# Attention and adapters on one core: the residual of nine row tiles is turned back by TensorE instead of by a transposing DMA

## The chip, the core and the metric

The kernel runs on one core of a Trainium2 chip. The metric is the device time of one execution in microseconds (us). Five engines work side by side, each with its own instruction queue: PE (TensorE, matrix products into PSUM; PEld are its weight loads), DVE (VectorE), ACT (ScalarE), POOL (GpSimd) and SP (SyncE). Here POOL only builds some constants and issues the input loads, SP issues stores and, before the change, transposing DMAs. Engines wait for one another through semaphores.

## What is computed

```python
def _attn_ref(q, k, v):                      # each (8, 12, 448, 64)
    scores = (1 / np.sqrt(64)) * np.matmul(q, k.transpose(0, 1, 3, 2))
    attn = np.maximum(scores, 0.0) ** 2 / 448
    return np.matmul(attn, v)

x = attn_out.transpose(0, 2, 1, 3).reshape(3584, 768)

def _moe_ref(x, w_gate, A, B):               # 8 experts of rank 16, the best 2 of each row
    logits = x @ w_gate
    # w: softmax over the two largest logits of a row
    # delta[row] = sum over its two experts e of w * (x[row] @ A[e]) @ B[e]
    return x + delta
```

So the output is the attention result x (3584 rows of 768) plus a small correction; x itself has to reach the output, row by row. It is this last part, the residual, that the change is about.

## The kernel before, in words

**Attention.** For each of 8 batches the 12 heads are worked in 3 "quads" of four heads. The inputs come by cast-loads from POOL's queue (`load`, L185, two DMAs of 112 KB for each q, k or v of a quad). TensorE turns q and k with an identity (`tp`, L313), a copy brings them to SBUF (`te`, L327 and L335). Then come 174 steps n: score products `qk` n (L452), relu n on ACT or DVE (L472, L474), squaring `sq` on DVE for two or three steps at a time (L489), and value products `pv` n (L520). Their result stands transposed, with the 64 head dimensions in the rows; copies `x` on ACT or DVE (L565) write it to `xt`, a tile of 128 rows by 6 blocks by 3584 columns in bf16. So x stands there turned: columns of `xt` are rows of the output.

**Adapters.** The 3584 output rows are 28 tiles of 128. Three tiles at a time go through the gate: `z` (L582, six products of each tile with the gate and A weights), a few small DVE steps (`gmax` to `gzp`), a transposing product `zt` in f32 (L644), and its copy `zT` (L661). Then each tile has two half tiles, `b` 2t and `b` 2t+1, each 384 columns wide, which sum residual and correction in a PSUM bank: three products of `xt` blocks with a bf16 identity (L728) turn x back, and a product of `zT` with B in f32 (L737; it is two instructions in the profile) adds the correction. A copy `o` (L773) on ACT or DVE brings the half to the tile `osb`, and a store `st` writes the rows (L783).

For nine of the 28 tiles (15 to 23, as three groups of three in `C["tg"]`) the kernel before does it otherwise: `turned` lets SP's queue issue six transposing DMAs for each group (L677, 18 in all), which write x turned back to a tile `xb`. Their half tiles then have only the product with B, and `o` is an add of PSUM and `xb` on DVE (L764):

```python
for x in range(0 if xb or xi else 3):
    nc.tensor.matmul(out=out(h)[:, x * 128 : x * 128 + 128],
                     lhsT=k.xt[:, 3 * h + x, c0 : c0 + 128], rhs=k.identb,
                     start=(x == 0), stop=False, skip_group_check=True)
...
nc.tensor.matmul(out=o, lhsT=T["zT", g0][:, zi], rhs=rhs,
                 start=xb is not None, stop=True, skip_group_check=True)
...
elif xb:
    nc.vector.tensor_add(osb()[...], out(h)[:, :W], T["xb", xb[1]][...])
...
else:
    cp(osb()[:, h * W : h * W + W], out(h)[:, :W])
```

**What sets the order.** No scheduler runs: the string `ORDER` lists all operations, with the engine after a colon (`:A`, `:D`) where there is a choice and the first PSUM bank after `@`. `ordered` walks through it and issues each operation on its engine, so the table fixes each engine's queue. Numbered words are n of `qk`, `relu`, `pv`, half tiles of `b` and `o`, and so on; words `f` are unnamed ones, mostly loads. Buffers come from pools of fixed size (`POOLS`), so a load on POOL can wait for PE to have finished with an older tile; a load also waits for the landing of the DMA issued eight before it.

TensorE works in two shapes here: `tp`, `qk` and `pv` address 64x64 quarters of its array, `z`, `zt` and `b` the whole. I call `b`, `z` and `zt` 128-row work, and a stretch of them between two 64-row operations a run.

Of the kernel before, what the change touches and what calls it, by code (L numbers as in the profile page):

```python
# [30 lines left out]
PARTS.update({7: ((0, 322, 1, (0, 1, 2)), (322, 448, 4, (0, 1, 2)))})  # L31


C = dict(late=6, xi=(), om=(), merge_x=0, sqp=((999, (2, 2, 3)),), om2=(), fl=(), gf=(), ai=4, tg=((15, 3), (18, 3), (21, 3)), sp=(), xbdur=1.45, bx=8, xh=2, apart=3, apcap=1, gl=(3, 1), tqlat=2.0)
GROUP = 2688
POOLS = dict(qT=5, a=11, zp=2, zT=3, osb=4, w=3, q=5, k=5, v=8, xb=3)


ORDER = """
f4 f3 f1 f0 f2 f6 f5 f8 f7 f11 f9 f10 f84@0 f12 f88 f85@2 f90 f89 f13 f87@4 qk0@6 f91 qk1@0 relu0:D qk2@2 f14  # L40
relu1:A qk3@4 relu2:D relu3:A tp2@6 f17 qk4@0 te2 relu4:A qk5@2 qk6@4 sq2 tp3@6 f16 relu5:A f86@0 te3 relu6:A
sq0 qk7@0 f15 qk8@2 qk9@6 relu7:A tp4@4 relu8:D relu9:A f18 qk10@0 te4 qk11@2 relu10:A qk12@6 sq4 tp5@4 f19
relu11:A qk13@0 relu12:A te5 tp6@2 f26 sq9 relu13:A qk14@4 qk15@6 tp7 relu14:A f23 sq7 pv0@0 pv1 pv2 relu15:A
pv3 qk16@4 te6 pv4 pv5 f20 relu16:A pv6 qk17@6 x13:D pv7@2 relu17:A qk18@4 sq11 f22 pv8 pv9 x12:A qk19@6
relu18:A pv10 qk20@0 relu19:D f21 pv11 relu20:A pv12 pv13 qk21@4 sq16 x27:A qk22@6 f27 qk23@0 relu21:A aw1@3
sq14 relu22:A f33 x26:D relu23:A qk24@4 tp8@6 ae1 f25 relu24:A sq18 qk25@0 qk26@2 tp9 relu25:A f55 pv14@4 pv15
pv16 te8 relu26:A pv17 qk27@0 f31 pv18 pv19 relu27:A pv20 sq23 qk28@2 qk29@6 x41:A f28 qk30@0 x40:D relu28:A
aw0@5 sq25 relu29:A f29 relu30:A qk31@2 ae0 tp10@6 tp11 f32 relu31:A sq21 qk32@4 qk33@0 relu32:A te10 pv21@2 f30
pv22 pv23 relu33:A qk34@4 sq30 qk35@6 relu34:A qk36@0 f37 relu35:D relu36:A qk37@4 pv24 pv25 relu37:A pv26 sq32
f35 qk38@6 tp12@0 pv27 relu38:A tp13 qk39@4 f43 x55:A te12 qk40@6 x54:A z0@3 relu39:A sq35 qk41@0 f34 z1  # L50
relu40:A qk42@4 relu41:D z2 relu42:A f38 qk43@6 gmax0 tp14@0 relu43:A sq28 qk44@4 tp15 f42 relu44:A gd0 qk45@6
gu0 te14 relu45:A qk46@4 f50 gt0 sq39 qk47@0 relu46:A pv28@6 pv29 pv30 gsg0 pv31 f24 relu47:A qk48@4 pv32 gw0
pv33 sq44 f48 pv34 relu48:A qk49@0 gzp0 x69:A f36 tp18@4 sq37 relu49:A tp19 pv35@2 zt0@7 zt1 zt2 x68:A f41 te18
qk50@0 zT0:A pv36 pv37 relu50:A qk51@6 sq46 pv38 pv39 f47 relu51:A pv40 qk52@4 qk53@0 pv41 relu52:A x82:D tp16@6
tp17 relu53:A te16 qk54@4 b2@2 relu54:A f44 sq49 qk55@0 o2:A qk56@6 qk57@4 relu55:A relu56:D b0@2 f49 x83:A
relu57:D qk58@0 o0:A qk59@6 f39 relu58:A z3@3 z4 sq51 relu59:A qk60@4 qk61@0 z5 f40 sq56 relu60:A b4@2 relu61:A
gmax3 qk62@6 f46 sq58 b1@4 relu62:A gu3 gd3 qk63@0 o4:A gt3 f65 sq42 qk64@6 gsg3 o1:A b3@5 relu63:A gw3 gzp3
b5@2 f51 relu64:A sq60 zt3@4 zt4 o3:A zt5 pv42@0 o5:A pv43 st2 qk65@6 zT3:A sq53 pv44 pv45 relu65:A qk66@2 st4
pv46 pv47 pv48 relu66:A tp20@4 st0 qk67@6 x96:D tp21 x97:A te20 f53 pv49@2 relu67:A pv50 qk68@0 pv51 pv52 sq63
relu68:A pv53 f66 pv54 pv55 qk69@4 qk70@6 x110:A relu69:D qk71@0 relu70:A f45 b6@2 x111:D relu71:A qk72@4 o6:D  # L60
tp22@6 relu72:A sq65 qk73@0 tp23 pv56@2 relu73:A pv57 f74 qk74@4 te22 pv58 pv59 relu74:A pv60 qk75@0 f79 pv61
sq67 pv62 relu75:A qk76@6 b8@4 f64 relu76:A x124:D qk77@0 x125:A sq70 tp24@6 relu77:A tp25 qk78@2 f59 z6@5 te24
relu78:A qk79@0 z7 relu79:A f52 o8:D qk80@2 qk81@6 sq72 z8 relu80:A b10@4 f54 gmax6 relu81:A sq77 qk82@0 tp26@2
o10:A tp27 qk83@6 relu82:A gd6 gu6 f56 b7@4 te26 relu83:A qk84@0 gt6 f70 o7:D qk85@2 gsg6 relu84:A qk86@6 gw6
sq74 b9@4 relu85:A pv63@0 pv64 relu86:A gzp6 pv65 qk87@2 pv66 sq79 pv67 relu87:A pv68 pv69 zt6@5 zt7 x138:D zt8
x139:A qk88@6 qk89@2 o9:A zT6:D qk90@0 relu88:A relu89:D st8 tp28@4 tp29 relu90:A f80 qk91@6 te28 pv70@2 pv71
relu91:A pv72 pv73 qk92@0 sq84 f60 pv74 pv75 relu92:A pv76 qk93@4 b14@6 x153:D x152:A f58 relu93:A sq81 qk94@0
tp30@2 o14:A tp31 pv77@4 relu94:A pv78 f77 qk95@6 te30 pv79 pv80 relu95:A pv81 qk96@0 pv82 f57 sq91 pv83
relu96:A qk97@2 b11@6 relu97:D x166:A f67 b12@7 x167:A o11:A sq93 qk98@0 st10 o12:A qk99@2 qk100@4 relu98:A
relu99:D b13@6 st6 relu100:A z9@7 sq88 qk101@0 o13:A tp32@2 qk102@4 relu101:A tp33 st12 b15@6 f62 sq86 relu102:A  # L70
qk103@0 o15:A te32 f61 qk104@4 relu103:A z10 z11 sq100 relu104:A qk105@2 f69 pv84@0 pv85 pv86 relu105:A gmax9
qk106@4 sq95 pv87 f72 pv88 relu106:A pv89 pv90 qk107@2 x181:A f63 gd9 qk108@4 gu9 relu107:D x180:A b16@6
relu108:A gt9 f81 qk109@0 o16:D gsg9 pv91@2 pv92 relu109:A pv93 gw9 sq105 qk110@4 pv94 pv95 relu110:A f78 pv96
qk111@0 gzp9 pv97 relu111:A x195:D zt9@6 zt10 qk112@4 f75 sq98 x194:A zt11 b17@7 relu112:A zT9:D qk113@0 o17:A
sq102 pv98@2 qk114@4 relu113:A pv99 st16 tp36@6 pv100 tp37 relu114:A pv101 st14 qk115@0 te36 pv102 pv103
relu115:A pv104 tp34@4 f83 tp35 sq109 qk116@6 x209:A qk117@0 x208:A b20@3 relu116:A f68 te34 b22@2 relu117:A f71
sq114 o20:A qk118@6 qk119@4 qk120@0 relu118:A b21@3 f73 sq112 o22:A b23@6 relu119:A o21:D sq107 st20 relu120:A
z12@7 qk121@2 qk122@4 relu121:A z13 relu122:D z14 o23:A qk123@0 pv105@2 gmax12 pv106 relu123:A qk124@4 gd12
pv107 gu12 pv108 gt12 sq116 pv109 relu124:A pv110 pv111 qk125@0 f82 b18@6 gsg12 relu125:A gw12 x223:D x222:A
qk126@4 f76 o18:D qk127@0 relu126:A b19@3 gzp12 sq121 relu127:A zt12@2 zt13 zt14 qk128@6 pv112@4 o19:D pv113  # L80
relu128:A qk129@0 pv114 zT12:D st18 pv115 pv116 relu129:A sq123 pv117 pv118 st22 tp38@2 qk130@6 x236:A tp39
qk131@0 xb90 relu130:A b24@4 te38 relu131:A tp42@6 sq119 xb93 tp43 x237:A qk132@2 b25@0 relu132:A te42 b28@1
xb91 o24:A o25:A sq128 qk133@2 o28:A qk134@6 tp40@4 sq126 relu133:A xb94 pv119@0 tp41 pv120 relu134:A pv121 te40
qk135@2 pv122 pv123 st24 relu135:A pv124 pv125 qk136@6 qk137@4 x251:D x250:A b29@2 sq130 relu136:A xb92 b26@3
relu137:A sq135 o29:A qk138@0 qk139@6 o26:A qk140@4 st28 relu138:A z15@2 relu139:D z16 xb108 z17 relu140:A
qk141@0 gmax15 pv126@6 pv127 relu141:A gd15 pv128 gu15 qk142@4 gt15 sq133 xb111 pv129 pv130 gsg15 pv131
relu142:A qk143@0 pv132 gw15 b27@3 gzp15 x264:A xb95 x265:D relu143:A zt15@2 zt16 zt17 sq137 pv133@4 o27:A
qk144@6 tp44@0 zT15:A pv134 st26 tp45 relu144:A qk145@2 pv135 te44 pv136 xb109 relu145:A pv137 qk146@6 pv138
pv139 sq140 relu146:A z18@0 xb112 b30@1 x279:A sq142 z19 x278:A qk147@2 qk148@6 o30 qk149@4 xb110 relu147:A z20
sq144 b32@1 relu148:A relu149:A b33@2 gmax18 qk150@6 o32 qk151@4 relu150:A b31@3 gu18 o33 relu151:A gd18 qk152@6  # L90
sq149 st32 b34@1 relu152:A gt18 o31 gsg18 qk153@4 qk154@6 gw18 o34 relu153:A st30 b35@2 gzp18 relu154:A xb113
qk155@4 o35 pv140@0 relu155:A pv141 sq151 qk156@6 pv142 pv143 relu156:A qk157@2 qk158@4 xb126 pv144 pv145
relu157:D relu158:A pv146 tp46@6 tp47 x293:A x292:D qk159@4 qk160@2 xb129 relu159:A zt18@1 te46 zt19 zt20 z21@0
relu160:A z22 sq156 zT18:A qk161@4 qk162@6 xb127 qk163@2 relu161:A b40@1 sq147 relu162:A z23 sq158 relu163:A
xb130 qk164@4 pv147@6 pv148 relu164:A pv149 pv150 o40 qk165@2 pv151 pv152 relu165:A pv153 sq154 qk166@4 st34
b41@1 relu166:A gmax21 xb128 x307:A gu21 qk167@2 gd21 sq163 pv154@4 x306:A pv155 pv156 relu167:A pv157 pv158
qk168@6 gt21 o41 pv159 gsg21 pv160 gw21 b36@2 st40 x320:A gzp21 x321:A sq161 b38@3 relu168:A xb131 zt21@1 sq165
zt22 zt23 qk169@4 zT21:A pv161@6 pv162 pv163 relu169:A pv164 o38 qk170@0 pv165 pv166 o36 relu170:A pv167 b37@3
x335:D sq168 x334:A qk171@4 qk172@0 qk173@6 relu171:A z24@2 o37 z25 relu172:A st36 sq170 b46@3 relu173:A b47@4
o46 b39@5 sq172 b44@3 o47 z26 o39 st46 pv168@0 gmax24 pv169 pv170@6 gd24 pv171 st38 x338:A gu24 pv172@4 gt24 o44  # L100
pv173 x343:A x339:A b45@0 gsg24 x346:A gw24 gzp24 b42@7 x347:D x342:D zt24@1 o45 zt25 zt26 b43@6 zT24:D st44 o42
z27@0 b52@1 o43 gmax27 st42 gd27 gu27 b53@3 gt27 o52:A gsg27 b50@2 gw27 gzp27 o53:D zt27@4 b51@5 st53 o50:A
b48@3 o51:D zT27:A st50 b49@2 o48:D b54@3 o49:A st49 b55@2 o54:D st54 o55:D st55
"""


# [37 lines left out]

def build(k=None, c=C):

# [808 lines left out]
```

## Time and profile before

| What | Value |
|---|---|
| time, median of 3 runs (lowest, highest) | 182.27 us (181.3, 183.01) |
| the profiled execution | 181.68 us |
| its span, first to last instruction | 179.6 us |
| granted TensorE clock | 1.00 throughout |
| PE copies of x through the identity (L728) | 114 products, 219 ns each (median) |
| PE product with B (L737) | 112 instructions, 514 ns each (mean) |
| score products (L452), value products (L520) | 756 each |
| transposing DMAs (L677) | 18, 3.2 us from issue to landing (median) |
| DVE adds of `xb` (L764) | 18, 549 ns each |
| copies of a half tile (L773) | 26 on ACT (529 ns), 12 on DVE (553 ns) |
| POOL's loads (L185) | 142 DMAs, about 0.63 us each to issue, 4.9 to 5.0 us to landing |

Durations in such a profile are from an instruction's start to its end. Products on PE are pipelined: the next one starts long before the first has ended, so a product of "219 ns" takes much less of PE's time, and what it costs is seen from one start to the next. "Busy" is the union of such stretches. The chain of work that ended last follows the last instruction back, at each step to what released it or to the instruction before it on its engine.

### The profile page before, as it was taken

To read this page: it belongs to the slowest core of one execution; us is meant where nothing else is said; L and a number is where in the kernel's file an instruction comes from. 1 tells how busy PE (TensorE), PEld (TensorE's weight loads), DVE (VectorE), ACT (ScalarE), POOL (GpSimd) and SP (SyncE) were. 2 spreads that over 40 slices of the span, in tenths; PEclk is the share of its full clock that TensorE was granted. 3 is DMA by queue.
4 is the path that set the end of the run, shared out by engine and by line. 5 is a ranking of instruction groups with operands and counts; after the bars stand their busy time and mean duration, and the time that the engine had idled before them with its cause. 6 is when DMAs were issued, how large, how long until landed. Compare 5 with 4: busy or idle time off the path is not lost.

```text
span 179.6 us, 7694 instructions
## 1 busy us (share of the span) xinstructions
PE 165.1 (92%) x3366; PEld 99.2 (55%) x3366; DVE 163.5 (91%) x254; ACT 156.2 (87%) x240; POOL 90.7 (50%) x155
## 2 busy tenths in 40 slices
PE   7887998888899999999979899999999999999990
PEld 2445476454535665646646465655666557576650
DVE  0699999999989999999999899999999999999831
ACT  3399999999999999999998999999999899993120
POOL 7999997988869377850966867250000000000000
PEclk9999999999999999999999999999999999999999
DMA  4999999999999999994699999988495663515644
GB/s 90 126 170 188 164 112 183 164 180 178 202 180 152 186 303 166 175 166 130 84 176 299 197 185 268 237 118 222 113 171 149 45 223 63 189 42 211 230 194 158
DMA packets 33985, 30.49 MB, mean 170 GB/s; under 512 B 11488, under 2 KB 30432, under 8 KB 33952
## 3 DMA queue, kind: packets, MB, share of 16 engines
q0 software_dynamic: 22000, 17.03, 65.7%
q1 hardware_dynamic: 11376, 11.90, 22.1%
q10 hardware_dynamic: 576, 1.08, 1.6%
q8 instruction: 26, 0.43, 0.9%
q14 instruction: 7, 0.06, 0.1%
HBM read 33.84 MB, written 11.01 MB: 250 GB/s over the span
## 4 chain that ended last, share of the span: by engine, by line
PE 44%; ACT 16%; DMA 16%; POOL 15%; issue 4%; DVE 2%; ACTq 0%; POOLq 0%
PE ps L737 17%; ACT a L472 14%; DMA q<-in_q_dram 9%; PE ps L452 9%; PE ps L520 8%; POOL k L185 5%; PE ps L582 4%; POOL v L185 4%; DMA B<-in_moe_B_dram 4%; POOL q L185 3%; PE ps L728 3%; DMA k<-in_k_dram 3%; PE ps L313 2%; ACT osb L773 2%; PE ps L644 1%
## 5 line engine op out<-in xcount | busy, mean ns | idle before, releaser
L472 ACT ACTIVATE a<-ps 128x896 bf16<-128x896 f32 (+3 forms) x158 | 132.7, 961 | 3.3 <-PE ps L452 3.0
L489 DVE TENSOR_TENSOR a<-a 128x1792 bf16<-128x1792 bf16 (+4 forms) x75 | 88.5, 1193 | 0.0
L452 PE MATMUL ps<-qT 64*64 64x448 bf16 (+2 forms) x756 | 57.9, 345 | 4.5 <-ACT a L472 3.3
L737 PE MATMUL ps<-B,zT 128*128 128x384 f32 x112 | 47.5, 514 | 0.3 <-DMA B<-in_moe_B_dram 0.3
L520 PE MATMUL ps<-a,v 64*64 64x448 bf16 (+2 forms) x756 | 44.3, 330 | 0.8 <-ACT a L472 0.4
L452 PEld LDWEIGHTS <-qT 64*64 64x64 bf16 x756 | 25.3, 106 | 31.9 <-issue 22.9
L185 POOL DMA_DIRECT2D k<-in_k_dram x46 | 27.8, 629 | 16.3 <-PE ps L452 7.1
L185 POOL DMA_DIRECT2D v<-in_v_dram x48 | 28.8, 621 | 8.1 <-PE ps L452 3.8
L185 POOL DMA_DIRECT2D q<-in_q_dram x48 | 29.4, 639 | 3.5 <-DMA v<-in_v_dram 1.5
L520 PEld LDWEIGHTS <-v 64*64 64x64 bf16 x756 | 22.6, 106 | 7.9 <-issue 2.7
L327 DVE COPY qT<-ps 128x1792 bf16<-128x1792 bf16 x21 | 22.8, 1084 | 0.7 <-ACT a L472 0.4
L565 ACT CAST xt<-ps 128x448 bf16<-128x448 f32 (+2 forms) x37 | 19.4, 560 | 2.6 <-PE ps L520 2.3
L773 ACT COPY osb<-ps 128x384 f32<-128x384 f32 x26 | 13.1, 529 | 7.4 <-PE ps L737 5.6
L737 PEld LDWEIGHTS ps<-B,zT 128*128 128x128 f32 x112 | 17.3, 190 | 3.7 <-DMA B<-in_moe_B_dram 0.4
L474 DVE TENSOR_SCALAR a<-ps 128x896 bf16<-128x896 f32 (+1 forms) x16 | 16.9, 1069 | 0.9 <-PE ps L452 0.9
L313 PEld LDWEIGHTS <-q 64*64 64x64 bf16 x672 | 10.4, 112 | 6.9 <-issue 3.3
L582 PEld LDWEIGHTS <-xt 128*128 128x128 bf16 x168 | 10.5, 98 | 5.7 <-issue 4.7
L582 PE MATMUL ps<-awg,xt 128*128 128x136 bf16 x168 | 13.5, 223 | 0.0
L728 PEld LDWEIGHTS <-xt 128*128 128x128 bf16 x114 | 8.0, 98 | 9.9 <-issue 8.1
L313 PE MATMUL ps<-identb,q 64*64 64x64 bf16 x672 | 10.9, 197 | 2.3 <-DMA q<-in_q_dram 1.1
L728 PE MATMUL ps<-identb,xt 128*128 128x128 bf16 x114 | 12.7, 220 | 0.2
L565 DVE CAST xt<-ps 128x448 bf16<-128x448 f32 (+2 forms) x17 | 9.6, 570 | 0.2 <-PE ps L520 0.2
(47 smaller groups left out, 97.9 us busy)
## 6 DMA issues: line engine op xcount, KB each, us to landing
out_dram<-osb SPq DMA_DIRECT2D x25, 384.0 KB, 4.2
q<-in_q_dram POOLq DMA_DIRECT2D x48, 112.0 KB, 5.0
v<-in_v_dram POOLq DMA_DIRECT2D x48, 112.0 KB, 4.9
k<-in_k_dram POOLq DMA_DIRECT2D x46, 112.0 KB, 4.9
out_dram<-osb ACTq DMA_DIRECT2D x2, 384.0 KB, 2.3
B<-in_moe_B_dram POOLq DMA_DIRECT2D x1, 384.0 KB, 6.6
xb<-xt SPq DMA_TRANSPOSE x18, 3.2
a_raw<-in_moe_A_dram POOLq DMA_DIRECT2D x1, 192.0 KB, 5.4
```

What stands on the lines that cost most here:

```text
L185: nc.gpsimd.dma_start(out=t[g * PH : g * PH + PH], in_=k.qkv[w][b, g, :, 2 * q : 2 * q + 2, :])
L313: nc.tensor.transpose(k.ps_b[sl * PH : sl * PH + PH, o.banks[g], (w * J + j) * PH : (w * J + j) * PH + PH], source(w, j)[r, sl], k.identb[ ...
L327: nc.vector.tensor_copy(t.rearrange("p g w x -> p g (w x)"), k.ps_b[:, m.banks[0] : m.banks[0] + 2, : 2 * S])
L452: nc.tensor.matmul(out=bank(o, sl)[g * PH : g * PH + PH, at : at + w].rearrange("k (j p) -> k j p", j=J), lhsT=t[r, g, 1, j * PH : j * PH ...
L472: nc.scalar.activation(out, flat(qk_ops[n], w), ACTF.Relu, scale=k.relu_scale)
L474: nc.vector.tensor_scalar(out, flat(qk_ops[n], w), k.relu_scale, 0.0, op0=ALU.mult, op1=ALU.max)
L489: nc.vector.tensor_mul(a, a, a)
L520: nc.tensor.matmul(out=bank(head, g)[sl * PH : sl * PH + PH, :w], lhsT=vn[r, sl, j * PH : j * PH + PH], rhs=T["a", g0][r, x + sl * width(n ...
L565: evac(w, lambda cp, g=g: cp(k.xt[:, g * QUADS + q, b * S + x0 : b * S + x1].rearrange("d (p j) -> d p j", j=J), bank(src, g)[:, :w].rearr ...
L582: nc.tensor.matmul(out=bank(zops[0])[:, t * ZW : t * ZW + ZW], lhsT=k.xt[:, do, 128 * tiles[t] : 128 * tiles[t] + 128], rhs=k.awg[:, do, : ...
L728: nc.tensor.matmul(out=out(h)[:, x * 128 : x * 128 + 128], lhsT=k.xt[:, 3 * h + x, c0 : c0 + 128], rhs=k.identb, start=(x == 0), stop=Fals ...
L737: nc.tensor.matmul(out=o, lhsT=T["zT", g0][:, zi], rhs=rhs, start=xb is not None, stop=True, skip_group_check=True,)
```

## The change

`C["tg"]` becomes empty, so that no tile goes through `turned`: all 28 tiles have their three identity products on PE in each half and a copy instead of the add. `POOLS["xb"]` goes from 3 to 1 (no tile is taken from it any more). The `ORDER` table is another one: the 18 words `xb` are gone, the 18 words `o30` to `o47` get an engine (17 times D, once A), and most other words stand in another place, among them the loads. No other line differs.

```diff
-C = dict(late=6, xi=(), om=(), merge_x=0, sqp=((999, (2, 2, 3)),), om2=(), fl=(), gf=(), ai=4, tg=((15, 3), (18, 3), (21, 3)), sp=(), xbdur=1.45, bx=8, xh=2, apart=3, apcap=1, gl=(3, 1), tqlat=2.0)
+C = dict(late=6, xi=(), om=(), merge_x=0, sqp=((999, (2, 2, 3)),), om2=(), fl=(), gf=(), ai=4, tg=(), sp=(), xbdur=1.45, bx=8, xh=2, apart=3, apcap=1, gl=(3, 1), tqlat=2.0)
-POOLS = dict(qT=5, a=11, zp=2, zT=3, osb=4, w=3, q=5, k=5, v=8, xb=3)
+POOLS = dict(qT=5, a=11, zp=2, zT=3, osb=4, w=3, q=5, k=5, v=8, xb=1)
...
-pv3 qk16@4 te6 pv4 pv5 f20 relu16:A pv6 qk17@6 x13:D pv7@2 relu17:A qk18@4 sq11 f22 pv8 pv9 x12:A qk19@6
+qk16@2 te6 pv3 pv4 relu16:A pv5 f21 qk17@4 pv6 sq11 pv7@6 relu17:A qk18@2 pv8 f19 relu18:A qk19@4 sq16 pv9 pv10
...
-pv139 sq140 relu146:A z18@0 xb112 b30@1 x279:A sq142 z19 x278:A qk147@2 qk148@6 o30 qk149@4 xb110 relu147:A z20
-sq144 b32@1 relu148:A relu149:A b33@2 gmax18 qk150@6 o32 qk151@4 relu150:A b31@3 gu18 o33 relu151:A gd18 qk152@6
+relu145:A pv137 qk146@0 pv138 pv139 sq140 relu146:A qk147@4 b30@2 x278:A sq142 z18@3 x279:A z19 relu147:A o30:D
+qk148@0 qk149@6 relu148:A z20 sq144 b32@2 relu149:A qk150@4 qk151@0 gmax18 relu150:A b31@6 o32:D gd18 relu151:A
...
-z27@0 b52@1 o43 gmax27 st42 gd27 gu27 b53@3 gt27 o52:A gsg27 b50@2 gw27 gzp27 o53:D zt27@4 b51@5 st53 o50:A
-b48@3 o51:D zT27:A st50 b49@2 o48:D b54@3 o49:A st49 b55@2 o54:D st54 o55:D st55
+o43:D b47@7 zT24:A st42 z27@6 b52@1 gmax27 gd27 o47:D b53@0 gu27 o52:A st46 gt27 gsg27 b50@7 gw27 o53:D gzp27
+st53 b51@4 o50:A b48@5 o51:D st50 zt27@4 b49@2 zT27:D o48:D b54@3 o49:A st49 b55@2 o54:D st54 o55:A st55
```

The loads up to B in the order in which POOL issues them (letter, batch.quad; "rest" is the second part of the first k; "aw" the weights of gate and A; "sel" a constant that POOL builds itself):

```
before  q0.0 rest q0.1 k0.1 q0.2 k0.2 k1.0 q1.0 v0.0 v0.1 q1.1 k1.2 aw k1.1 sel v0.2 v1.0 v1.2 q1.2 q5.0 q2.1
        q2.0 k2.0 k2.1 v1.1 q3.0 k2.2 q3.2 q2.2 k3.0 v2.2 k4.1 B
after   q0.0 rest q0.1 k0.1 q0.2 k0.2 k1.0 v0.0 q1.0 v0.1 q2.1 aw sel v0.2 q1.1 k1.1 q1.2 k1.2 k2.1 v1.0 k2.0
        k2.2 q2.0 q4.0 v1.1 v1.2 k3.0 k5.2 q3.0 k3.1 q2.2 q3.1 B
```

## The prediction

> **What bounds the kernel now.** I read the busy line of the page first, then the busy time by stage, then the chain of work that ended last, then single rows.
>
> ```profile
> PE 165.1 (92%) x3366; PEld 99.2 (55%) x3366; DVE 163.5 (91%) x254; ACT 156.2 (87%) x240; POOL 90.7 (50%) x155
> ```
>
> Three engines look equally full, so the average does not say which one sets the end. The stages do. I cut the span at the start of the score products qk100 (91.0 us), qk120 (110.6), qk147 (139.8), qk173 (159.9) and at the last output copy (about 176). Columns: stretch, its length, then PE, PEld, DVE, ACT, POOL busy, granted clock, DMA share, GB/s.
>
> ```profile
> 30.20:55.50 25.30, 21.85 (x547) 12.75 (x545) 24.49 (x32) 24.99 (x37) 21.05 (x36) 1.00 1.17 180
> 55.50:77.70 22.20, 21.69 (x469) 13.03 (x467) 21.98 (x36) 22.20 (x35) 16.31 (x28) 1.00 1.13 196
> 91.00:110.60 19.60, 18.16 (x387) 10.81 (x383) 18.55 (x26) 18.78 (x29) 14.21 (x25) 1.00 1.16 233
> 110.60:139.80 29.20, 29.10 (x586) 17.90 (x574) 28.45 (x44) 28.93 (x46) 4.22 (x8) 1.00 0.86 167
> 139.80:159.90 20.10, 20.09 (x376) 12.39 (x378) 19.89 (x42) 18.70 (x34) 0.00 (x0) 1.00 0.44 123
> 159.90:176.00 16.10, 15.36 (x192) 9.89 (x181) 12.28 (x33) 5.08 (x13) 0.00 (x0) 1.00 0.51 199
> ```
>
> Until 77.7 ACT has no gap and PE has some; from 110.6 on PE has none (29.10 of 29.20, 20.09 of 20.10), and at the end ACT and DVE are plainly short of work while PE is not. The chain agrees: between 108 and 175 us it consists almost wholly of PE pieces, before 94 us of ACT, POOL and DMA. All the work that the change adds is PE work, and the 18 changed half tiles all start behind 138.6 us.
>
> **What is removed.** The 18 transposes and the rows that use them:
>
> ```profile
> L677 SPq DMA_TRANSPOSE xb<-xt x18: 1202/1241/2175, 121.1 to 155.9; - x18
> L764 DVE TENSOR_TENSOR osb<-ps,xb x18: 537/549/558, 140.0 to 168.2; 128x384 f32<-128x384 f32 x18
>   PEld ps L737: 0.3, 1
> ```
>
> The transposes take SP's queue (1.24 us each) and 3.2 us from issue to landing, in a stretch where the DMA engines are 44 to 86% busy; no engine's wait names them. SP issues only stores beside them, and the products that wait for an output buffer show one wait of 0.3 us, on DVE's add. Taking the transposes away is worth 0 to 0.3 us; I take 0, because from 139.8 to 159.9 PE has 0.01 us of idle time to give back. The cover is PE's own full queue: were PE not full there, the 0.3 would count. The 18 adds (549 ns) become plain copies; the order table puts 17 of them on DVE (copy row: 553 ns) and one more on ACT (529 ns). The table also moves one relu (about 1.0 us) and one zT copy (0.55) from DVE to ACT and one xt copy (0.62) back: all told DVE loses about 1.5 us of 163.5 and ACT gains as much on 156.2. Neither sets the end behind 139.8, where both have gaps.
>
> **What is added.** Three identity products per half tile, 18 x 3 = 54, with 54 weight loads. Their busy rows (219 ns a product) overlap, so I price them by starts. A timeline of PE around half tiles without and with them (start, duration, what):
>
> ```profile
> 142.57 0.91 PE L737 MATMUL ps<-B,zT 128*128 128x384 f32 x2
> 143.42 0.33 PE L452 MATMUL ps<-qT 64*64 64x322 bf16 x4
> 143.68 0.91 PE L737 MATMUL ps<-B,zT 128*128 128x384 f32 x2
> ```
>
> ```profile
> 99.80 0.34 PE L728 MATMUL ps<-identb,xt 128*128 128x128 bf16 x3
> 99.98 0.86 PE L737 MATMUL ps<-B,zT 128*128 128x384 f32 x2
> 100.77 0.38 PE L452 MATMUL ps<-qT 64*64 64x448 bf16 x4
> ```
>
> and from the chain, four half tiles without them in a row, then two with them:
>
> ```profile
> 161.06 2.65 PE ps L737 x8
> ...
> 172.82 0.70 PE ps L737 x2
> 173.69 0.70 PE ps L737 x2
> ```
>
> Alone between two 64-row products, a half tile without them costs 143.42 - 142.57 = 0.85 us, with them 100.77 - 99.80 = 0.97: 0.12 more. Inside a run of 128-row work it is 2.65 / 4 = 0.66 against 173.69 - 172.82 = 0.87: 0.21 more. Counted in the order table of before, 8 of the 18 half tiles open a run and 10 stand inside one: 8 x 0.12 + 10 x 0.21 = 3.06 us of PE.
>
> Here a rule speaks against the change: the Trainium skill, "TensorE: Matmul & The Clock Gate", section "Back-to-back issue gap", says that a sustained stream of weight load and product pairs of 128 columns goes at about 81 ns a pair. By that, 54 pairs are an estimated 4.4 us. The rows give 40 to 70 ns a product, since part of each hides under the change of array shape; I take the rows, 3.06, and keep 4.4 for the upper end. Another rule speaks for it: "VectorE: DVE Perf Modes", section "Rules for kernel authors", says to transpose 128x128 on TensorE where PSUM will do as a destination and by the DMA crossbar otherwise. By it the change costs nothing; but by the stage rows TensorE is the one engine without a gap where these 18 stand and nobody waits for the transposes, so the rule does not hold here and the 3.06 stays.
>
> **What is moved.** All engines' orders are new. Changes between 64-row and 128-row work: 99 before, 105 after, so three more runs. A run costs 0.97 - 0.87 = 0.10 at its own half tile, and 0.12 at the score product before it (0.26 us between 143.42 and 143.68 against 0.14 us for such a group among its own kind at 146.30): 3 x 0.22 = 0.66 us. Behind qk120 stand 34 half tiles instead of 35 (16 gate products both times), and two of the three runs: 3.06 - 0.92 + 0.44 = 2.6 us more PE work behind 110.6. Before it 0.92 + 0.22 = 1.1 us more, all between qk100 and qk120, where PE has 19.60 - 18.16 = 1.44 us of gaps and, by the table, DVE has about 1.9 us less to do (two squarings come later). I take 0.2 of the 1.1 as exposed; bounds -0.5 (PE's gaps take it all and DVE's relief shows) and 1.1.
>
> The loads are reordered too. They run on POOL's queue at about 1.19 us each, so a place in the list is a time. Two of them end in waits of the chain:
>
> ```profile
> 44.23 6.55 DMA B<-in_moe_B_dram
> 50.83 0.91 PE ps L737 x2
> ...
> 88.52 5.31 DMA q<-in_q_dram
> 93.87 0.41 PE ps L313 x26
> ```
>
> B's load keeps its place in the list (31 loads ahead of it), but its first use now comes ahead of one more score product, 0.8 us of ACT's time earlier: 0 to 0.8 us more, I take 0.4, since ACT gets an xt copy to fill in. The q load of batch 1, third quad, ends a wait of 0.3 us of ACT at 32 us; two loads fewer stand ahead of it: 0.3 less. The k load of batch 1, second quad, moves back behind the selection matrix and one more load: issued near 21.8 instead of 18.2 us, landing some 4 us later at 25.4 to 26.7, while before it was used at 25.7: 0 to 1 us more, I take 0.5. The q load of 88 us (batch 5, second quad) now stands behind a load that needs a buffer freed at 82 us and two more, but is used about 1 us later: -0.8 to +1.0, I take 0. These waits stand one behind the other, and a delay at the first gives the next load as much time, so they don't add up: of 0.6 I take 0.2 together, from -1.1 (only the gains) to +2.0. What such a wait delays: the score products queued behind the transposing products on PE, and ACT's relus behind those.
>
> **Sum.** 2.6 + 0.2 + 0.2 = +3.0 us on the span of 179.6, so 182.6; with the 2.1 us around it (181.68 - 179.6) 184.7 for the profiled execution. That execution lies 0.6 below the median of 182.27, so on the median: 185.3 us. The ends, with all parts at once: 2.6 - 0.5 - 1.1 = +1.0 (183.3), and 3.9 (by the 81 ns: 2.6 + 1.3) + 1.1 + 2.0 = +7.0 (189.3).
>
> **Rivals.**
> - *The loads decide against it.* The k load of batch 1 and the q load of batch 5 both land late and nothing absorbs it: 2.6 + 1.1 + 2.0 = +5.7 at most, +4.2 in the middle: about 186.5. For it: the chain runs through exactly these loads. Against: each is bounded by about 1 us, and the q load of batch 1 comes earlier.
> - *The new order wins the idle time back* (the other side). The gaps of the fullest engine after 30 us are 25.30 - 24.99 = 0.31, 0, 0.04 (77.7 to 91.0) and 19.60 - 18.78 = 0.82: 1.2 us in all, where loads come late. If they all go, and the 1.1 us of moved work fits PE's own gaps, the end is 2.6 - 1.2 = +1.4: 183.7, within 1% of before. It decides from 0.8 us on (1% is 1.8 us). To be faster by 1% it would have to win 4.4 us, more than these gaps hold, unless the first 30 us shrink too.
> - *DVE is the real limit* behind 139.8 (19.89 of 20.10). Then its 1.5 us less come out as a gain: 180.8, no change. Against: the adds become copies of the same length, nearly all on the same engine, and from 159.9 to 176 DVE has 3.8 us of gaps, PE 0.7.
> - *The change doesn't do what it says:* the transposes' absence lets stores out earlier and nothing else happens. The last store follows the last copy by the same rows, so 182.3.
>
> **How the numbers follow.** PE pays and the loads stay about even: 0.58, 184.0 to 186.5. Loads against it: 0.15, 185.5 to 188. Idle won back: 0.18, 182.7 to 184.1. DVE the limit or nothing happens: 0.05, 180.5 to 182.5. Faster by over 1%: 0.04. A measurement of this kernel can tell about 1% from no change, so 180.4 to 184.1 counts as the same: 0.18 + 0.05 and 0.03 of the first case, 0.26; slower 0.70; faster 0.04. The range, 183.0 to 187.5, leaves out about 0.1 on either side.
>
> **What would show it.** Right: L728 has 168 products instead of 114; PE is over 98% busy from qk120 to the last half tile and this stretch is 2 to 3.5 us longer than the 65.4 of before (110.6 to 176); DVE and ACT have more gaps there than before. Wrong: PE gaps behind qk120 (then a wait, not work, is the cause), qk120 starting before 109 us (the order won more than I give it), or after 112 us (a load is late; the waits for L313 name it).

## The result, and the profile after

| | before | after |
|---|---|---|
| median of 8 executions each (lowest, highest) | 181.85 us (180.91, 183.01) | 183.62 us (182.87, 184.72) |
| ratio | 1 | 1.0102, 95% interval 1.0064 to 1.0140 |
| the profiled execution | 181.68 us | 183.49 us |
| its span | 179.6 us | 181.3 us |

The changed kernel is slower by 1.8 us in the medians, at the edge of what this measurement can tell from no change; the forecast was +3.0 us on the span and 185.3 us. In ratios, executions over 1.5% above the fastest of their kernel are left out; in one experiment below four of six lay there, and they are told there as they are. All lines of after stand one lower than before (L727 for L728, L736 for L737, and so on), since the diff leaves one line less.

From the page of the changed kernel, the busy time of the engines and the groups of the half tiles:

```profile
PE 168.8 (93%) x3420; PEld 100.7 (56%) x3420; DVE 162.3 (90%) x252; ACT 157.7 (87%) x242; POOL 90.2 (50%) x155
...
L736 PE MATMUL ps<-B,zT 128*128 128x384 f32 x112 | 48.5, 514 | 0.1
...
L772 ACT COPY osb<-ps 128x384 f32<-128x384 f32 x27 | 13.5, 535 | 6.2 <-PE ps L736 6.2
L727 PE MATMUL ps<-identb,xt 128*128 128x128 bf16 x168 | 18.8, 221 | 0.1
...
L772 DVE COPY osb<-ps 128x384 f32<-128x384 f32 x29 | 15.6, 552 | 3.1 <-PE ps L736 3.0
```

There are 168 identity products instead of 114, and 56 copies where there were 38 copies and 18 adds. PE's busy time grew by 3.7 us, ACT's by 1.5, DVE's fell by 1.2. Where, the busy time by stage tells: the span of after cut at its own starts of qk100 (91.4), qk120 (110.7), qk147 (137.5), qk173 (162.4) and at its last output copy (178.4); columns as in the prediction.

```profile
91.40:110.70 19.30, 19.24 (x397) 11.13 (x389) 18.73 (x27) 19.30 (x31) 12.89 (x22) 1.00 1.13 213
110.70:137.50 26.80, 26.80 (x560) 15.83 (x560) 25.99 (x41) 26.78 (x43) 2.60 (x5) 1.00 0.53 142
137.50:162.40 24.90, 24.90 (x461) 15.78 (x459) 22.83 (x45) 21.59 (x39) 0.00 (x0) 1.00 0.22 84
162.40:178.40 16.00, 15.47 (x178) 9.91 (x166) 10.26 (x30) 5.06 (x14) 0.00 (x0) 1.00 0.43 167
```

From 110.7 to 162.4 PE has no gap at all. DVE's gaps behind qk120 are 0.8 + 2.1 + 5.7 = 8.6 us, where they were 4.8. The first of the four rows is the surprise: from qk100 to qk120 PE has 0.06 us of gaps instead of 1.44, and this stage did not get longer but shorter. ACT has no gap in it either (19.30 of 19.30; 18.78 of 19.60 before). The stages overlap in kind of work (the new table puts less between qk120 and qk147 and more behind), so only the sums from qk120 on compare.

The chain of work that ended last, in the last 10 us of after: nothing but PE, one half tile every 0.87 us as before, and the last copy.

```profile
174.29 0.17 PE ps L727 x3
174.46 0.70 PE ps L736 x2
175.16 0.11 PE ps L643
175.27 0.17 PE ps L727 x3
175.44 0.70 PE ps L736 x2
...
177.91 0.48 ACT osb L772
```

Here is where the 1.65 us between the two spans (179.61 and 181.26) stand, by the starts of instructions in the two traces:

| stretch | before | after | difference |
|---|---|---|---|
| start to qk100 | 90.94 | 91.42 | +0.48 |
| qk100 to qk120 | 19.70 | 19.25 | -0.45 |
| qk120 to the end of the last copy | 65.22 | 67.72 | +2.50 |
| last copy to the end of the span | 3.76 | 2.87 | -0.89 |

The third row is the forecast's own (2.6). The second and the fourth are gains that it did not have; each has experiments below.

### The profile page after: what moved, and what is told of

Read it like the earlier page. It is cut to its first block, busy times and chain, and to the rows that moved or that the text cites. A ratio compares the mean times of both kernels' runs of the same rounds, so it can differ in the third digit from the quotient of the medians.

```text
span 181.3 us, 7757 instructions
## 1 busy us (share of the span) xinstructions
PE 168.8 (93%) x3420; PEld 100.7 (56%) x3420; DVE 162.3 (90%) x252; ACT 157.7 (87%) x242; POOL 90.2 (50%) x155
## 4 chain that ended last, share of the span: by engine, by line
PE 57%; ACT 16%; POOL 10%; DMA 10%; issue 3%; DVE 3%; ACTq 0%; POOLq 0%
PE ps L736 19%; ACT a L471 12%; PE ps L451 12%; PE ps L519 11%; PE ps L727 6%; DMA k<-in_k_dram 6%; POOL q L184 5%; PE ps L581 5%; DMA B<-in_moe_B_dram 4%; PE ps L312 2%; ACT osb L772 2%; POOL k L184 2%; POOL v L184 1%; PE ps L643 1%; ACT xt L564 1%
## 5 line engine op out<-in xcount | busy, mean ns | idle before, releaser
L488 DVE TENSOR_TENSOR a<-a 128x1792 bf16<-128x1792 bf16 (+3 forms) x75 | 88.4, 1196 | 0.5 <-ACT a L471 0.4
L451 PE MATMUL ps<-qT 64*64 64x448 bf16 (+2 forms) x756 | 60.2, 349 | 5.5 <-DVE a L473 1.9
L736 PE MATMUL ps<-B,zT 128*128 128x384 f32 x112 | 48.5, 514 | 0.1
L519 PE MATMUL ps<-a,v 64*64 64x448 bf16 (+2 forms) x756 | 45.3, 332 | 0.3
L564 ACT CAST xt<-ps 128x448 bf16<-128x448 f32 (+2 forms) x36 | 18.4, 551 | 2.8 <-PE ps L519 2.5
L727 PE MATMUL ps<-identb,xt 128*128 128x128 bf16 x168 | 18.8, 221 | 0.1
L727 PEld LDWEIGHTS <-xt 128*128 128x128 bf16 x168 | 11.2, 97 | 13.2 <-issue 10.6
L772 DVE COPY osb<-ps 128x384 f32<-128x384 f32 x29 | 15.6, 552 | 3.1 <-PE ps L736 3.0
L736 PEld LDWEIGHTS ps<-B,zT 128*128 128x128 f32 x112 | 16.9, 191 | 0.3 <-DMA B<-in_moe_B_dram 0.3
L473 DVE TENSOR_SCALAR a<-ps 128x896 bf16<-128x896 f32 x15 | 16.2, 1087 | 0.7 <-PE ps L451 0.4
L581 PEld LDWEIGHTS <-xt 128*128 128x128 bf16 x168 | 10.5, 98 | 4.8 <-issue 4.0
L312 PEld LDWEIGHTS <-q 64*64 64x64 bf16 x672 | 9.8, 111 | 3.6 <-issue 1.9
```

What stands on the lines that cost most here:

```text
L451: nc.tensor.matmul(out=bank(o, sl)[g * PH : g * PH + PH, at : at + w].rearrange("k (j p) -> k j p", j=J), lhsT=t[r, g, 1, j * PH : j * PH ...
L473: nc.vector.tensor_scalar(out, flat(qk_ops[n], w), k.relu_scale, 0.0, op0=ALU.mult, op1=ALU.max)
L488: nc.vector.tensor_mul(a, a, a)
L519: nc.tensor.matmul(out=bank(head, g)[sl * PH : sl * PH + PH, :w], lhsT=vn[r, sl, j * PH : j * PH + PH], rhs=T["a", g0][r, x + sl * width(n ...
L564: evac(w, lambda cp, g=g: cp(k.xt[:, g * QUADS + q, b * S + x0 : b * S + x1].rearrange("d (p j) -> d p j", j=J), bank(src, g)[:, :w].rearr ...
L581: nc.tensor.matmul(out=bank(zops[0])[:, t * ZW : t * ZW + ZW], lhsT=k.xt[:, do, 128 * tiles[t] : 128 * tiles[t] + 128], rhs=k.awg[:, do, : ...
```

## The experiments

Each ratio is to the kernel before on the same chip (medians there 181.31, 181.76 and 180.97 us in the three batches). The edits are shown in excerpts: lines are shortened to the part that matters, "..." stands for more lines of the same kind, and where `tg` changes, the pool `xb` and the words `xb` of the table change with it. Beside it I use two stretches of each profile, qk100 to qk120 and qk120 to the last copy: they repeat to 0.03 us between kernels that share order and loads there, while whole executions differ by 1 to 2 us, mostly from the first 30 us.

| kernel | ratio | qk100 to qk120 | qk120 to last copy | last copy to end |
|---|---|---|---|---|
| before | 1 | 19.70 | 65.22 | 3.76 |
| products in the old order | 1.0196 | 19.56 | 68.29 | 2.86 |
| transposes in the new order | 1.0027 | 19.25 | 64.81 | 3.70 |
| after without the products | 0.9986 | 19.25 | 64.79 | 2.87 |
| before without transposes | 0.9946 | 19.37 | 65.21 | 2.87 |
| before, six stores split | 0.9937 | 18.69 | 65.23 | 2.87 |
| after, products twice | 1.0305 | 19.27 | 70.73 | 2.87 |
| before, q load earlier | 0.9992 | 18.70 | 65.24 | 3.72 |
| before, split and q earlier | 0.9920 | 18.70 | 65.24 | 2.87 |
| after, two stores split | 1.0138 | 19.25 | 67.73 | 3.23 |
| after, q load later | (two groups) | 20.64 | 67.72 | 3.18 |
| after as it is, again | 1.0152 | 19.25 | 67.71 | 2.86 |

### What do the 54 products cost, and does the order matter?

**The old order with the products**: the table of before, without the transposes.

```diff
-tg=((15, 3), (18, 3), (21, 3))
+tg=()
-pv139 sq140 relu146:A z18@0 xb112 b30@1 x279:A sq142 z19 x278:A qk147@2 qk148@6 o30 qk149@4 xb110 relu147:A z20
+pv139 sq140 relu146:A z18@0 b30@1 x279:A sq142 z19 x278:A qk147@2 qk148@6 o30:D qk149@4 relu147:A z20
...
```

> The order table of before, word for word, without the 18 transposes; the 18 half tiles get their three identity products and a plain copy on DVE instead of the add. Theory (PE pays for the products behind qk120, and the new order won part of it back): 8 x 0.12 + 10 x 0.21 = 3.06 us more than before, ratio 1.017, all of it between qk120 and the last half tile, and the wait for the q load of batch 5 (1.1 us at its transposing products) is still there. Rival A (the new order table, not the products, makes the change slower): ratio 1.000 to 1.005. Rival B (the transposes' transfers cost something themselves): less than 2.5 us more.

Measured: 185.30 us (183.75 to 187.41), ratio 1.0196 (1.0143 to 1.0249). From qk120 to the last copy 68.29 - 65.22 = 3.07 us more; all 18 half tiles stand there. The profile was also 2.6 us behind that of before at relu 30 and 1.9 us at qk100, with the granted clock at 0.66 between 15 and 20 us. Nothing ahead of qk100 was edited.

**The changed kernel without the products.** Nine row tiles (15 to 23) get only their correction, x is missing in them.

```diff
-for x in range(0 if xb or xi else 3):
+for x in range(0 if xb or xi or 15 <= tl < 24 else 3):
-start=xb is not None, stop=True,
+start=xb is not None or 15 <= tl < 24, stop=True,
```

> The changed kernel without the 54 identity products: nine row tiles lack x in their output, nothing else differs. Theory: 2.9 us less than the changed kernel, ratio to before 0.994, and the same as the new order with transposes within 0.3 us, since the transposes cost nothing. Rival B (transposes cost something): clearly less than the new order with transposes, by 0.5 us or more.

Measured: 181.04 us (180.23 to 181.89), ratio 0.9986 (0.9954 to 1.0018). From qk120 on 67.72 - 64.79 = 2.93 us less, as expected. The ratio expected, 0.994, was missed, and against the new order with the transposes (1.0027, below) it is 0.7 us less, which was the sign named for transposes that cost something. The next section finds where.

**The changed kernel with the products twice** (54 more, on the same banks):

```diff
-for x in range(0 if xb or xi else 3):
+for x in [0, 1, 2] * (0 if xb or xi else 2 if 15 <= tl < 24 else 1):
```

> The changed kernel with the three identity products of the 18 half tiles issued twice, the second time starting the sum anew: 54 more products on PE, nothing else. Theory (PE's products are what the change costs, at about 0.06 to 0.07 us each once they stand inside a run): 18 x 0.17 to 18 x 0.21 = 3.1 to 3.8 us more than the changed kernel, so a ratio to before of about 1.029. Rival A (the products are hidden and the order sets the time): within 1 us of the changed kernel, ratio up to 1.016.

Measured: 186.77 us (186.56 to 188.31), ratio 1.0305 (1.0261 to 1.0349), so 2.0% (3.7 us) over after's 1.0102, or 1.5% over the 1.0152 of a second measurement of after on the same chip (below); from qk120 on 70.73 - 67.72 = 3.01 us, a little under the 3.1 to 3.8 expected. The chains of the three kernels show one half tile each; first after without the products (a stretch of half tiles without them, from its chain):

```profile
164.46 2.13 PE ps L736 x6
```

that is 2.13 / 3 = 0.71 each; then after, and then with the products twice:

```profile
163.54 0.17 PE ps L727 x3
163.71 0.70 PE ps L736 x2
164.41 0.17 PE ps L727 x3
164.58 0.70 PE ps L736 x2
```

```profile
165.84 0.34 PE ps L727 x6
166.17 0.70 PE ps L736 x2
166.88 0.34 PE ps L727 x6
167.21 0.70 PE ps L736 x2
```

Each three products are another 0.17 us of PE, and nothing beside them takes it up. So behind qk120 the 54 products cost 2.9 to 3.1 us in either order and the same again when doubled: it is PE time and no wait. Half tile by half tile, by the start of PE's next instruction with the products and without, one that opens a run costs 0.13 us more (mean of 8 in the old order, 10 in the new) and one inside a run 0.20 (10 and 8); the other half tiles behind them change by 0.003 us at most, and the second set costs 0.17 everywhere. The medians are a blunter tool: the same pairs of kernels differ by 4.5 us in the old order (1.0196 to 0.9946) and by 2.1 in the new (1.0102 to 0.9986). In the profiles most of what the old order has above 3.1 stands ahead of qk100, where the two kernels do the same work (it starts at 92.87 and 90.52 us); why is not known.

**The new order with the transposes**: the table of after, `tg` as before, the 18 transposes put behind the copies that they need.

```diff
-tg=()
+tg=((15, 3), (18, 3), (21, 3))
-pv110 qk124@4 pv111 st20 b18@6 relu124:A f75 gu12 gd12 gt12 x222:A x223:D qk125@2 qk126@4 gsg12 relu125:A b19@0
+pv110 qk124@4 pv111 st20 b18@6 relu124:A f75 gu12 gd12 gt12 x222:A xb90 xb108 x223:D xb93 xb111 qk125@2 qk126@4
...
```

> The order table after the change, but with the transposes kept: the 18 transposing DMAs are put in right behind the copies they need, and the 18 half tiles have no identity products and an add on DVE. Theory: the new order alone is a gain, as its loads come in better time: of the 18 half tiles 10 open a run and 8 stand inside one in this table, so 10 x 0.12 + 8 x 0.21 = 2.9 us less than the changed kernel, some 1.1 us less than before, ratio 0.994. Rival A (the new order is worse): at or above before, 1.000 to 1.010.

Measured: 181.86 us (180.60 to 183.23), ratio 1.0027 (1.0003 to 1.0051). The expected 0.994 was missed: the table is no gain by itself. From qk120 on it is 0.4 us shorter (64.81 for 65.22), but the medians do not show it.

### What was the removal of the transposes worth?

**The kernel before without its transposes**: the 18 adds are copies of PSUM alone, so again nine row tiles lack x; table and products as before.

```diff
-tg=((15, 3), (18, 3), (21, 3))
+tg=()
-for x in range(0 if xb or xi else 3):
+for x in range(0 if xb or xi or 15 <= tl < 24 else 3):
-start=xb is not None, stop=True,
+start=xb is not None or 15 <= tl < 24, stop=True,
```

> The kernel before without its 18 transposes; the adds are plain copies on DVE, so nine row tiles lack x in their output. Theory: the transposes are hidden, so no difference, ratio 0.997 to 1.002. Rival B: 0.5 us or more less, ratio below 0.997.

Measured: 180.04 us (179.17 to 182.96), ratio 0.9946 (0.9919 to 0.9974). "No difference" (0.997 to 1.002) was missed; this is the rival's number. The stretch from qk120 to the last copy is untouched (65.21), as the prediction had it. But the time from the last copy to the end fell from 3.76 to 2.87 us. At the end of the program (L950 before, L949 after) SP looks at one DMA semaphore after another. These are SP's rows on that line in before, from 177.0 to 178.9 us, where the last store has landed at 177.75 (form: engine, operation, count: shortest/median/longest ns, first and last start):

```profile
L950 SPq EVENT_SEMAPHORE  x8: 28/28/28, 177.8 to 178.7; - x8
L950 SPq DRAIN  x2: 7/10/13, 178.8 to 178.8; - x2
```

and in after, from 179.5 to 180.6, where the last store has landed at 180.30 (the first of the three rows, at 179.57, stands ahead of that):

```profile
L949 SPq EVENT_SEMAPHORE  x3: 28/28/28, 179.6 to 180.4; - x3
L949 SPq DRAIN  x2: 7/7/7, 180.4 to 180.5; - x2
```

In before SP makes all eight looks behind the last landing, and is done 1.0 us later (177.75 to 178.76); in after six of the eight are over by then, and it is done 0.15 us later (180.30 to 180.45). The traces show why, by the semaphore that each landing raises: the DMAs of the store queues (29 stores, the transposes, two small loads) use eight semaphores in turn. With 49 of them the last store has the first semaphore that SP looks at, with 31 the seventh. Of the 1.0 us in before, 0.47 is one pause between two looks (177.94 to 178.40).

If that is the cause, other DMAs in the place of the transposes must do the same. **The kernel before with its first six stores as two halves each**, so 55 DMAs and the seventh semaphore, transposes kept:

```diff
-{"SP": nc.sync, "ACT": nc.scalar}[e].dma_start(out=k.out[c0 : c0 + 128, c1:c2], in_=T["osb", tl][:, c1:c2])
+for x0, x1 in ((c1, W), (W, c2)) if tl < 6 else ((c1, c2),):
+    {"SP": nc.sync, "ACT": nc.scalar}[e].dma_start(out=k.out[c0 : c0 + 128, x0:x1], in_=T["osb", tl][:, x0:x1])
```

> The kernel before, transposes and all, but the stores of the first six row tiles go out as two halves each: six more DMAs on SP's queue, which turns the round of the eight semaphores that these queues use, so that the last store's semaphore is the seventh of the eight that SP looks at before the program ends, as in the changed kernel, and not the first. Theory C (0.9 us of what the transposes cost is this end: with 18 more DMAs the last store's semaphore is looked at first, and SP still has all the other looks ahead of it when it lands): from the last output copy to the end of the span 2.9 us instead of 3.8, 0.8 us less in all, ratio 0.9955. Rival B (the transposes' transfers themselves cost it): no less than before, ratio 0.999 to 1.003.

Measured: 180.57 us (179.41 to 182.42), ratio 0.9937 (0.9911 to 0.9963); last copy to end 2.87. From 178.0 to 178.5, behind a last landing at 178.18, SP has two looks left instead of eight:

```profile
L951 SPq EVENT_SEMAPHORE  x2: 27/28/28, 178.2 to 178.3; - x2
L951 SPq DRAIN  x2: 7/10/13, 178.3 to 178.4; - x2
```

So all that taking the transposes away brings (0.9946) comes as well with every transpose in place (0.9937). In its profile qk100 to qk120 is shorter too (18.69), by the load of the next section, so a part of the ratio may be that.

**The changed kernel with two stores split** goes the other way: 33 DMAs, and the last store has the first semaphore again (the same edit with `tl < 2`).

> The changed kernel; the stores of row tiles 0 and 1 go as two halves each, so that 33 instead of 31 DMAs of the store queues stand before the end and the last store again uses the first of the eight semaphores in the order in which SP looks at them. Theory C (the end of the program costs about 0.9 us more when the last store's semaphore is looked at first): last copy to span end 3.7 us instead of 2.87, ratio 1.0102 + 0.0047 = about 1.015. Rival (the stores' own timing made the difference, not the semaphore's place): 2.9 us and 1.010.

Measured: 183.70 us (183.09 to 184.12), ratio 1.0138 (1.0095 to 1.0181), and beside it, on the same chip:

> The changed kernel without any edit, on the same chip as the two beside it, to compare them with: ratio within 1.0064 to 1.014.

183.84 us (182.78 to 185.40), ratio 1.0152 (1.0100 to 1.0205), a little above what was expected. Last copy to end 3.23 against 2.86. Half of the expectation holds: all eight looks now stand behind the last landing (179.36), and SP is done 0.52 us behind it instead of 0.15. This is its row from 179.0 to 180.0:

```profile
L950 SPq EVENT_SEMAPHORE  x8: 28/28/28, 179.4 to 179.8; - x8
```

Eight looks in 0.46 us, without a pause. So the place of the semaphore is worth 0.37 us. The pause is a second effect, which the other two kernels with 49 DMAs share with before (3.70 and 3.72 in the table) and this one does not; what makes it stays open. A difference of 0.37 us is below what the two ratios can tell apart.

### The q load of 88 us

In before the transposing products of batch 5, second quad, wait for their q. From the waits of before between 84 and 112 us (engine, line, what ended the wait, us in total, times, longest):

```profile
PEld L313 <- DMA q<-in_q_dram: 1.2, 1, 1.2
...
PE ps L313 <- DMA q<-in_q_dram: 0.9, 1, 0.9
```

Its second half landed at 93.83, while the first of the products began at 92.77: 1.06 late. In after it landed at 92.36, 1.81 before it was needed, and the only row of that line in the same window is this one:

```profile
PEld L312 <- issue: 0.5, 1, 0.5
```

**The kernel before with that load (f58) ahead of the one before it in POOL's list:**

```diff
-x139:A qk88@6 qk89@2 o9:A zT6:D qk90@0 relu88:A relu89:D st8 tp28@4 tp29 relu90:A f80 qk91@6 te28 pv70@2 pv71
+x139:A qk88@6 qk89@2 o9:A zT6:D qk90@0 relu88:A relu89:D st8 tp28@4 tp29 relu90:A f58 f80 qk91@6 te28 pv70@2
...
```

> The kernel before with one word of its table moved: the load of q for batch 5, second quad, goes ahead of the loads of k for batch 7 and v for batch 4 on POOL's queue. Theory (half of what the new order won back is this one wait): the load is issued at 83 instead of 88 us, lands before the transposing products want it at 92.8, and the stretch from qk100 to qk120 gets 0.8 to 1.4 us shorter: ratio 0.992 to 0.996. Rival (the wait is taken up by others anyway): 0.998 to 1.002.

Measured: 181.54 us (180.11 to 183.45), ratio 0.9992 (0.9968 to 1.0016). The wait is gone (landed 2.7 us ahead of need) and qk100 to qk120 takes 18.70 instead of 19.70, yet the median hardly moves: not the 0.992 to 0.996 expected, but what the rival said (0.998 to 1.002). **With the six stores split as well:**

> The kernel before with both edits, the six stores in halves and the q load moved up. Theory: both gains add, 1.6 to 2.2 us, ratio 0.988 to 0.991: faster than both kernels. If the load's wait was hidden, only the 0.8 us at the end are left, ratio 0.9955.

Measured: 179.96 us (179.32 to 181.46), ratio 0.9920 (0.9892 to 0.9949): the fastest kernel of the study, ahead of both, with the split alone at 0.9937 within its interval, and short of the 0.988 to 0.991 of two gains that add. One reason for the small effect is in the profiles: with the old list the load was late by 1.06, 0.92 and 0.73 us in three kernels (before, products in the old order, before without transposes), but 0.23 early in the fourth (six stores split), which then shows 18.69 too. So with one list it can be late or in time. How late the first part runs does not decide it alone: the products in the old order were the latest of all at qk100 (92.87), and their load was late too. From the interval, the wait is worth 0.6 us or less in the median.

**The changed kernel with that load two places later:**

```diff
-tp30@0 o14:A tp31 pv77@6 relu94:A pv78 f58 qk95@4 te30 pv79 pv80 relu95:A pv81 pv82 qk96@2 f63 sq91 pv83 qk97@0
-x166:A b11@4 relu96:A relu97:D f71 b12@5 x167:A sq93 o11:A f74 qk98@2 o12:A qk99@0 st10 qk100@6 relu98:A
+tp30@0 o14:A tp31 pv77@6 relu94:A pv78 qk95@4 te30 pv79 pv80 relu95:A pv81 pv82 qk96@2 f63 sq91 pv83 qk97@0
+x166:A b11@4 relu96:A relu97:D f71 f58 b12@5 x167:A sq93 o11:A f74 qk98@2 o12:A qk99@0 st10 qk100@6 relu98:A
```

> The changed kernel with one load moved back by two places in the list: the q load of batch 5, second quad, is issued near 89.8 instead of 87.4 us and should land near 94.7, about 0.5 us or more after its transposing products could start (94.2), as in the kernel before. If the moved load was worth what the profile suggests (about 1 us between qk100 and qk120), ratio about 1.013 to 1.016. If such a wait is absorbed behind it or mostly hidden, 1.010 to 1.012.

Measured: two executions at 182.84 and 184.35 us, four at 187.16 to 187.90; no ratio is given for two groups so far apart. The one at 184.35 is profiled: the load's second half lands 0.77 us after the first of its products began, which had itself waited 0.7 us on PE for the first half, and qk100 to qk120 takes 20.64 instead of 19.25, 1.4 us more, which nothing behind gives back. The waits of that kernel between 84 and 112 us:

```profile
PEld L312 <- DMA q<-in_q_dram: 2.0, 2, 1.3
...
PE ps L312 <- DMA q<-in_q_dram: 0.6, 1, 0.6
```

> The same kernel as the one with the q load of batch 5, second quad, moved back by two places, once more, for a second profile: of its six executions two took 182.8 and 184.4 us and four took 187.2 to 187.9, and only one of the former is profiled. If this one takes about 187 us, the theory (this load is late and its wait is what costs) expects the additional 3 us between qk100 and qk120, as a longer wait of the transposing products for this load; the rival expects them elsewhere (another load, or the first 30 us). If it takes about 184, the question stays open.

Measured: 184.93 us; the load is 0.91 late and the stretch 20.89, so 1.6 us more. It is not one of the longer executions. What takes the other 3 us in those four stays open.

## Why the prediction was right, and where it was too high

The time, 183.62 us, lies in the range (183.0 to 187.5), near its lower end. The mechanism of the likeliest case, "PE pays", is what happened behind qk120. The number is not that case's: it is 1.7 us under the 185.3, below the case's own 184.0 to 186.5, and among the times given to "idle won back" (182.7 to 184.1) and to "the same" (up to 184.1). By its steps:

| step | forecast | measured |
|---|---|---|
| products | 3.06 | 2.93 (new order), 3.07 (old order) |
| order behind qk120: one half tile less, two more runs (-0.92 + 0.44) | -0.48 | 64.79 - 65.22 = -0.43 |
| qk100 to qk120: exposed part of 1.1 us more work | +0.2 | 19.25 - 18.69 = +0.56 |
| the q load of 88 us | 0 (-0.8 to +1.0) | 18.69 - 19.70 = -1.01 in the profile |
| other loads, up to qk100 | +0.2 with the q load | +0.48 in the profile |
| last copy to end | 0 | -0.89 |
| span | +3.0 | 2.93 - 0.43 + 0.56 - 1.01 + 0.48 - 0.89 = +1.64 |
| around the span | 0 | medians 2.07 before, 2.25 after: +0.2 |
| before's median above its profiled execution | +0.6 (three executions) | 181.85 - 181.68 = +0.2 (eight) |

So the products and the order, the part that was reasoned through, are right to 0.1 us. The other terms of the span are off by +0.4 (qk100 to qk120), -0.7 (all loads together) and -0.9 (the end). That they leave the time within a range 4.5 us wide is in part luck.

**What held.** The price of a product from the starts of its neighbours, and its two sizes: 0.12 and 0.21 us a half tile were forecast, 0.13 and 0.20 measured. That a part "hides under the change of array shape" fits this; why it does was not tried. The two orders give 2.93 / 54 = 54 ns and 3.07 / 54 = 57 ns a product, the second set 56. The Trainium skill ("TensorE: Matmul & The Clock Gate", section "Back-to-back issue gap") gave 81 ns a pair, by estimate 4.4 us for 54; the measurement decides for the rows. The rule for transposing on TensorE ("VectorE: DVE Perf Modes", section "Rules for kernel authors") does not hold here, as the prediction said: on the engine without gaps the products cost 3 us, and the transposes (3.2 us to landing) delayed nothing between qk120 and the last copy (65.22 with them, 65.21 without). The signs named beforehand came as stated: L727 with 168 products, PE over 98% busy from qk120 to qk173, that stretch 2.5 us longer, qk120 at 110.67 between 109 and 112, more gaps on DVE and ACT.

**What failed.** The step "Taking the transposes away is worth 0 to 0.3 us; I take 0", and with it the sentence of the fourth rival that "the last store follows the last copy by the same rows". I had looked for engines that wait for the transposes, and found none, which was right; I had not looked behind the last copy, where 3.76 us of the span lie. Their number decides which semaphore the last store uses, and that was worth 0.9 us on the span and 0.5 to 0.6% in the medians. With -0.89 in place of the 0 the sum would have been +2.1, against 1.65 in the profiled executions and 1.8 in the medians.

**What was mis-sized.** The q load: -1.01 lies below the lower end of -0.8. I had taken its place in the list as later by more than its use; in the trace it is issued at 87.44 instead of 87.94 and used 1.4 us later (94.16 for 92.77). In the medians this is worth less than in the profile (0.9992 for the load alone). The exposed part between qk100 and qk120 was 0.56 and not 0.2: PE's gaps there had mostly been this one wait (0.53 are left of 1.44 when the load is earlier, with the six stores split), so with the load in time there was less room for the 1.1 us than I counted. Nor was DVE relieved: it has ten squarings in this stretch before and after, and is busy 18.73 us for 18.55. A rival was overlooked here: ACT has no gap in this stretch with the load in time (18.68 of 18.70 us, old order; 19.25 of 19.25, new order with the transposes) and has 0.57 us more to do, as much as the stretch grew. Whether PE's work or ACT's sets these 0.56 us was not tried apart. The k load of batch 1 did land 0.5 us late as forecast (26.92 for 26.42), but cost nothing: relu 25 and relu 30 are both 0.97 us behind before. B's load, taken at +0.4, gave 0.25 back (relu 50 is 0.87 us behind, relu 55 0.62). The tables also have 36 and 35 half tiles behind qk120, one more each than I counted, which leaves the difference as it was. The profiled execution lost its time earlier, with a lower granted clock in the third and fourth slice of the page's row (each 4.5 us):

```profile
PEclk9975999999999999999999999999999999999999
```

In the eight profiles with the new table qk100 starts between 90.49 and 91.68, in the six with the old between 90.52 and 92.87, so they do not show the +0.48 to be the change's. That the clock cost it was not shown either.

**The rivals.** That the loads decide against the change is refuted for this table (no wait for L312 on a load behind 84 us), but the mechanism is real: the same load two places later costs 1.4 to 1.6 us. That the new order wins idle time back is partly right: the q wait, and 0.4 us behind qk120; not more, since the table with the transposes kept is at 1.0027. DVE is not the limit behind qk120: its gaps nearly doubled there.

**What stays open.** In medians the new table without products (0.9986) is 0.4% slower than the old one without transposes (0.9946), though in their profiles it is 0.5 us faster from qk100 to the last copy (84.04 to 84.58). Of these 0.7 us, 0.4 lie around the span (medians 2.59 and 2.16 us); for the rest, and for the 0.5 that the profiles promise, there is only the part ahead of qk100, where single executions differ too much to show it. Nor was it found what the other 3 us of the four longer executions with the q load later are, or why in both profiles of that kernel the rows behind SP's looks take 0.3 us more than in after (3.18 in the table for 2.87), with the last store on the same semaphore.

## What to carry to other kernels

Price work added to a full engine from one start to the next in the same surroundings; that held to 5% here in two orders, and the same work doubled cost 3% less than the low end of what was expected. A piece of work for which no engine waits can still cost time where the program ends, so when DMAs are added or taken away, read the rows between the last landing and the end of the span in both kernels. Whether a load that is late in one profile costs anything in the median has to be tried, for in another execution it may be in time.

## What the runs showed of the hardware

- At the end of the program SP looks at DMA semaphores in a fixed order, 0.06 to 0.07 us apart. A last store on the first of eight cost 0.37 us more than one on the seventh, and in the three profiled kernels with 49 such DMAs (before, the transposes in the new order, the q load earlier) a pause of 0.44 to 0.47 us came on top. Splitting six early stores in two took both away: 2.87 us from the last copy to the end instead of 3.76, ratio 0.9937 (0.9911 to 0.9963).
- The time around the span differs from kernel to kernel: a median of 2.07 us in before, 2.25 in after, 2.41 with the transposes in the new order, 2.59 in after without the products. Single executions of after also stand at 3.2 to 3.5. What makes it so was not tried.
- The granted clock falls for a few us in the first 20 in some executions and not in others of the same kernel: in one profile of after it was 0.72 from 9.1 to 13.6 us and 0.52 from there to 18.1, in the other it was full. Of 41 executions of before, the 14 with a mean clock of 0.995 or more took 180.96 us on average, the 5 below 0.985 182.91.
